# Projected attention before a gated feed-forward layer: two-head blocks per visit, or one head at a time through block-diagonal operands

## Chip, core and metric

The kernel runs on one core of one Trainium2 chip. The metric is the device time of one execution in microseconds (us). Before the change the median of three runs is 549.61 us (547.75 to 552.11).

The core has five engines that work through their own instruction queues in order and wait for each other through semaphores: TensorE (PE, matmuls), ScalarE (ACT), VectorE (DVE), GpSimd (POOL) and SyncE (SP). In this kernel POOL issues the loads that change the type from fp32 to bf16, and SP issues the stores of the output and the transposing transfers ("turns").

## What is computed

```python
# q, k, v: [8 batches, 8 heads, 1024 tokens, 64]; E, F: [64, 1024]
k_proj = E @ k                                    # per batch and head, [64, 64]
v_proj = F @ v                                    # [64, 64]
scores = q @ k_proj.T / 8                         # [1024, 64]
attn = exp(scores - max) / (sum(exp(scores - max)) + 1e-9)
x = attn @ v_proj                                 # [1024, 64]; heads side by side: [8192, 512]
gate = sigmoid(x @ w_gate)                        # w_gate, w_val: [512, 1536]
out = (gate * (x @ w_val)) @ w_out                # w_out: [1536, 512]; out: [8192, 512]
```

The kernel leaves out the subtraction of the maximum; the scores of these inputs are small.

## The kernel before

**Tiling.** A batch is 1024 tokens. The attention works on two token halves of 512 laid over each other: a tile has 128 partitions, 64 for each half, and 512 columns. `Qb` holds q with tokens on partitions; four transposing transfers (`transpose_q`, one for each pair of heads `r`) make `qT`, with the 64 features of the two halves on 128 partitions. `eT` are the exponentials, with the 64 projected positions on partitions. `xT` is the attention's result with features on partitions; the feed-forward part reads it as its moving operand. It has one buffer for even and one for odd batches. A batch of the feed-forward part is two blocks of 512 tokens, and each block three pieces `K`, so a batch has six.

**Feed-forward part.** Each piece runs a chain for the gate (`g_chain`, banks GA and GC of PSUM) and one for the value (`v_chain`, VA and VC); each block ends with a chain for the output matrix (`o_chain`, OA and OC). The chains use a scheme with seven products for a two by two block matrix, with sums of operands prepared by DVE (`xs_sums`, `s_sums`). Their matmuls have 128x128 weights and 256 columns. Partial results are kept by ACT and added by DVE. The output tile `ost` has one buffer for each of four token groups. `evac` and `add_snap` write it, `stored` sends it to DRAM from SP in two pairs, and the next chain's `evac` has to wait until its pair has landed.

**Attention of batch b+1 beside the feed-forward part of batch b.** Four kinds of visit are put in between:

- `sc_visit`: scores of two head pairs, 64x64 blocks of the array, four matmuls of 512 columns beside each other, on banks GA, GC, XA and XB; ACT takes the exponential of each bank.
- `den_visit`: sums of the exponentials over the projected positions, by matmuls with a selection matrix (`dsel8`) on XA; DVE takes two reciprocals of 128x128 (L984) into `rdr`, a piece of `xu`.
- `spread`: SP writes the reciprocals to DRAM (L1153), and four transfers from POOL (L1168) read them back, each value repeated over 64 partitions, into `rb`, another view of `xu`.
- `xo_visit`: the outputs of two head pairs, again in 64x64 blocks; DVE multiplies each bank of 128x512 by the spread reciprocals and writes `xT` (`scaled`, L1184).

`next_kv` projects k and v for the batch after next on XA. `keep_kd` copies the projected k twice side by side, a transposing transfer puts it on both partition halves (`kpD`), and `vd_one` copies the projected v into each half of one of two `vpD`. `next_loads` then loads q, k and v of a later batch.

**What sets the order.** From the last part of batch 0 on, each operation is a task with an estimated duration, and matmuls that belong together form a group with a due time (`goal`). `arranged` replays the tasks with these durations and writes out one order for each engine. On the chip each engine follows this order and waits where a semaphore says so. A transfer that waits in SP's order holds back all that stand behind it.

Batches 0 and 1 run in other ways at the start of the kernel; the change leaves their mathematics as it is. The helpers through which all operations pass have single lines: matmuls are L378, activations L382, loads L396.

Of the kernel before, what the change touches and what calls it, by code (L numbers as in the profile page):

```python
# [12 lines left out]
P = 128  # L13
# [219 lines left out]
def bass_linformer_attn__then__ffn_glu_sigmoid_kernel(  # L233
# [18 lines left out]
    with contextlib.ExitStack() as es:  # L252
# [11 lines left out]
        def within(shape, dtype):  # L264
# [40 lines left out]
        kpd = sbuf("kpd", [64, H, 2, DH], BF16)  # L305
        kpD = sbuf("kpD", [P, H, DH], BF16)
        vpDs = [sbuf(f"vpD{i}", [P, H, DH], BF16) for i in range(2)]
        vpD = vpDs[0]
# [17 lines left out]
        rb = xu[:, :, :].rearrange("p n c -> p (n c)").rearrange(  # L326
            "p (r j h c) -> p r j h c", j=4, h=2, r=2
        )
        rdr = xu[:, 7, 0:256]
# [328 lines left out]
        def keep_v(bks, c0, engines, R=None):  # L658
            vv = vpD[:, :, :].rearrange("p (r h) d -> p r h d", h=2)
            width = 256 if R is None else 128  # L660
            for n, (h, g) in enumerate(((0, 0), (1, 1), (0, 1), (1, 0))):
                o = vv[64 * g : 64 * g + 64, pairs(R), h, :]
                i = bank[bks[h]][64 * h : 64 * h + 64, c0 : c0 + width].rearrange(
                    "p (r d) -> p r d", d=DH
                )
                ws = [("vpD", h, g, x, 0) for x in both(R)]
                if engines[n] == "ACT":
                    act(o, i, [], ws, b=bks[h])
                else:
                    dve(lambda e, o=o, i=i: e.tensor_copy(o, i), [], ws, b=bks[h])  # L670
# [24 lines left out]
        def VPD(R, n=0):  # L695
            return [("vpD", h, g, R, n) for h in range(2) for g in range(2)]
# [203 lines left out]
        def keep_kd(bk):  # L900
            act(
                kpd[:, :, :, :],
                bank[bk][0:64, :]
                .rearrange("p (h d) -> p h d", h=H)
                .unsqueeze(2)
                .to_broadcast([64, H, 2, DH]),
                [],
                ["kpd"],
                b=bk,
                t=0.95,  # L910
            )
# [3 lines left out]
                    kpD[:, :, :],  # L915
                    kpd[:, :, :, :].rearrange("p h g d -> p (h g d)"),
                ),
                r=["kpd"],
                w=[("kpD", 0), ("kpD", 1)],
                dma="kpD",  # L920
            )

        def vd_one(bk, g, n=1):
            act(
                vpDs[n][64 * g : 64 * g + 64, :, :].rearrange("p h d -> p (h d)"),
                bank[bk][64:128, :],
                [],
                [("vpD", h, g, R, n) for h in range(2) for R in range(2)],
                b=bk,
            )  # L930

        rd_v = [nc.dram_tensor(f"rd{b}", [P, 256], FP32, kind="Internal").ap() for b in range(B)]
        group = plan.group
        rb_keys = [("rb", c, rnd) for c in range(2) for rnd in range(2)]

        def attention(b):
# [44 lines left out]
            def rec(c):  # L981
                cc, bk = slice(c * P, (c + 1) * P), den_bank[0]
                dve(
                    lambda e: e.reciprocal((rden if b < 2 else rdr)[:, cc], bank[bk][:, cc]),  # L984
                    [],
                    [("rden", c, R) for R in range(2)] if b < 2 else [("rdr", c)]
                    + rb_keys
                    + ([("xu", n) for n in range(8)] if b == 2 else []),
# [57 lines left out]
            def xo_one(r, bks):  # L1046
                for g in range(2):
                    n = 2 * r + g
                    for c in range(2):
# [4 lines left out]
                            vpDs[(b - 1) % 2][kk, 2 * r + c, :],  # L1054
                            eT[kk, n, :],
                            VPD(r // 2, (b - 1) % 2) + [("eT", n)],
# [93 lines left out]
            def spread():  # L1150
                add(
                    "SP",
                    lambda e: e.dma_start(rd_v[b], rdr),  # L1153
                    r=[("rdr", c) for c in range(2)],
                    w=[("rd", b)],
                    dma="rd",
                    t=2.5,
                )
                for rnd in range(2):
                    for c in range(2):  # L1160
                        src = (
                            rd_v[b]
                            .rearrange("(g m) (o c) -> o g m c", g=8, o=1)[:, :, 2 * rnd + c, :]
                            .to_broadcast([64, 8, 256])
                        )
                        add(
                            "POOL",
                            lambda e, src=src, rnd=rnd, c=c: e.dma_start(  # L1168
                                rb[64 * c : 64 * c + 64, rnd, :, :, :].rearrange(
                                    "p j h c -> p (j h) c"  # L1170
                                ),
                                src,
                            ),
                            r=[("rd", b)],
                            w=[("rb", c, rnd), ("spread", c, rnd)],
                            dma=f"rb{c}{rnd}",
                            t=8.0,
                            )

            def scaled(r, g, bk):  # L1180
                n = 2 * r + g
                rnd, j = n // 4, n % 4
                dve(
                    lambda e: e.tensor_tensor(  # L1184
                        xT[s][:, r, :, 256 * g : 256 * g + 256],
                        bank[bk][:, :].rearrange("p (f c) -> p f c", f=2),
                        rb[:, rnd, j, :, :],
                        ALU.mult,
                    ),
                    [("rb", c, rnd) for c in range(2)],  # L1190
                    [("xT", s, r, 0, g), ("xT", s, r, 1, g)],
                    b=bk,
                )

            def sc_visit(goal, rs, banks):
                with group(goal, 0.22 * len(rs) + 0.2):
                    for i, r in enumerate(rs):
                        sc_one(r, banks[2 * i : 2 * i + 2])
                for i, r in enumerate(rs):
                    for g in range(2):  # L1200
                        exp_half(r, g, banks[2 * i : 2 * i + 2])

            def xo_visit(goal, rs, banks):
                with group(goal, 0.22 * len(rs) + 0.2):
                    for i, r in enumerate(rs):
                        xo_one(r, banks[2 * i : 2 * i + 2])
                for i, r in enumerate(rs):
                    for g in range(2):
                        scaled(r, g, banks[2 * i + g])

            def den_visit(goal, bk):
                den_bank.clear()
                with group(goal, 0.64):
                    den8(bk)
                rec(0)
                rec(1)
                spread()
# [6 lines left out]
                sc_visit=sc_visit,  # L1224
                xo_visit=xo_visit,
                spread_keys=[("spread", c, rnd) for c in range(2) for rnd in range(2)],
                den_visit=den_visit,
# [621 lines left out]
        start_loads()  # L1849
        constants()  # L1850
# [150 lines left out]

        def next_kv(b, goal):
            with group(goal, 1.83):
                kv(b, XA)
            keep_kd(XA)
            vd_one(XA, 0, (b - 1) % 2)
            vd_one(XA, 1, (b - 1) % 2)
# [9 lines left out]
        transpose_q([("kpD", 0)])  # L2017
# [10 lines left out]
        def next_loads(b, marker):  # L2028
            if b < B:
                load_q(b, (), marker)  # L2030
                load_k(b, [("kpD", 0), ("kpD", 1)], marker)
                load_v(b, (), marker)

        for b in range(1, B):
            n = attention(b + 1) if b + 1 < B else None
            late_ = 1 if b == 1 else 0
            more = b + 2 < B
            for u in range(6):
                K = 6 * b + u
                t0 = when(K)  # L2040
                if n is not None:
                    if b == 1 and u == 0:
                        for r in range(NR):
                            n["sc_visit"](9.0 + 3.0 * r, (r,), (XA, XB))
                        n["den_visit"](21.0, XA)
                        transpose_q(n["spread_keys"])
                    if b > 1 and u == 0:
                        n["sc_visit"](t0 - 1.0, (0, 1), (GA, GC, XA, XB))
                        if more:
                            transpose_q((), (0, 1))  # L2050
                    if b > 1 and u == 1:
                        n["sc_visit"](t0 - 1.0, (2, 3), (GA, GC, XA, XB))
                        if more:
                            transpose_q((), (2, 3))
                        n["den_visit"](t0 + 3.0, XA)
                    if u == late_ + 3:
                        if b > 1 and more:
                            next_kv(b + 2, t0 - 5.0)
                            next_loads(b + 3, n["spread_keys"])
                        n["xo_visit"](t0 - 1.0, (0, 1), (GA, GC, XA, XB))  # L2060
                        if b == 1:
                            next_kv(3, t0 + 4.0)
                            next_loads(4, n["spread_keys"])
                    if u == late_ + 4:
# [49 lines left out]
```

The softmax here doesn't subtract the row's maximum and nothing guards it: scores larger than these inputs give would overflow.

## Time and profile before

| what | value |
|---|---|
| median time | 549.61 us |
| span of the profiled execution | 545.3 us |
| PE busy | 512.6 us (94%) |
| DVE busy | 405.1 us (74%) |
| ACT busy | 351.6 us (64%) |
| POOL busy | 53.7 us (10%) |
| granted PE clock, mean | 0.977 of full speed |
| bytes moved by DMA | 69.41 MB, 127 GB/s on average |
| software queue (POOL) | 42.47 MB, 50.3% of the 16 DMA engines' time |
| hardware queue (SP) | 26.22 MB, 21.1% |

Busy time of PE is the union of its matmuls, which overlap in a pipeline. The profile's 40 slices are 13.6 us each, with busy time in tenths. A group's line gives the operation, output and inputs by name (pA and pF are PSUM banks, the letter and number of the bank left out), the shape, the count, busy us and mean ns, and the idle time before. A wait is put down to the engine or transfer that ended last. For a transfer the profile has the time from issue to landing.

### The profile page before, as it was taken

To read this page: it belongs to the slowest core of one execution; us is meant where nothing else is said; L and a number is where in the kernel's file an instruction comes from. 1 tells how busy PE (TensorE), PEld (TensorE's weight loads), DVE (VectorE), ACT (ScalarE), POOL (GpSimd) and SP (SyncE) were. 2 spreads that over 40 slices of the span, in tenths; PEclk is the share of its full clock that TensorE was granted. 3 is DMA by queue.
4 is the path that set the end of the run, shared out by engine and by line. 5 is a ranking of instruction groups with operands and counts; after the bars stand their busy time and mean duration, and the time that the engine had idled before them with its cause. 6 is when DMAs were issued, how large, how long until landed. Compare 5 with 4: busy or idle time off the path is not lost.

```text
span 545.3 us, 11320 instructions
## 1 busy us (share of the span) xinstructions
PE 512.6 (94%) x4668; PEld 403.1 (74%) x4677; DVE 405.1 (74%) x670; ACT 351.6 (64%) x644; POOL 53.7 (10%) x76
## 2 busy tenths in 40 slices
PE   5999999996999969999699996999999999999996
PEld 4545546784888748888488884887888888888885
DVE  3648789785697666877568765687797879786874
ACT  2564756872787636867368673686767866676762
POOL 9310200120102010020100201002000100000000
PEclk9999999998999989999899998999999999999999
DMA  9999999999996993459944799246812090111113
GB/s 157 199 200 199 155 213 196 141 208 142 135 230 130 156 238 63 121 87 133 226 74 122 82 150 239 48 128 88 150 44 78 21 191 32 40 40 40 40 40 115
DMA packets 81091, 69.41 MB, mean 127 GB/s; under 512 B 35088, under 2 KB 70160, under 8 KB 81040
## 3 DMA queue, kind: packets, MB, share of 16 engines
q0 software_dynamic: 37440, 42.47, 50.3%
q1 hardware_dynamic: 43600, 26.22, 21.1%
q8 instruction: 36, 0.59, 0.5%
q14 instruction: 15, 0.12, 0.1%
HBM read 72.88 MB, written 17.56 MB: 166 GB/s over the span
## 4 chain that ended last, share of the span: by engine, by line
PE 80%; DMA 13%; DVE 3%; ACT 1%; issue 1%; POOL 1%; SPq 0%; ACTq 0%; DVEq 0%; POOLq 0%
PE pA L378 44%; PE pF L378 36%; DMA out_dram<-ost 7%; DMA KVs<-in_v_dram 2%; DMA xu<-rd 2%; DMA rd<-xu 1%; DVE hT L1814 1%; DVE vsnap L1692 0%; ACT pF L1681 0%; DVE xT L820 0%; DVE ost L1425 0%; DVE hT L1289 0%; DVE xu L984 0%; POOL KVs L396 0%; POOL Qb L396 0%
## 5 line engine op out<-in xcount | busy, mean ns | idle before, releaser
L382 ACT ACTIVATE sig<-pA 128x512 f32<-128x512 f32 x126 | 75.1, 596 | 52.9 <-PE pA L378 52.3
L1768 DVE TENSOR_TENSOR sig<-pF,sig 128x512 f32<-128x512 f32 x84 | 57.8, 689 | 51.8 <-PE pF L378 26.9
L1681 ACT ACTIVATE pF<-pA 128x512 f32<-128x512 f32 x99 | 58.2, 589 | 33.5 <-PE pA L378 29.0
L1692 DVE TENSOR_TENSOR vsnap<-pF,vsnap 128x512 f32<-128x512 f32 x90 | 62.0, 689 | 20.1 <-ACT vsnap L382 11.4
L378 PE MATMUL pF<-wO,hT 128*128 128x256 bf16 (+1 forms) x400 | 58.6, 285 | 0.2 <-issue 0.2
L1814 DVE SCALAR_TENSOR_TENSOR hT<-sig,vsnap 128x512 bf16<-128x512 f32 x84 | 56.9, 683 | 0.9
L382 ACT ACTIVATE vsnap<-pA 128x512 f32<-128x512 f32 x84 | 50.1, 597 | 8.5 <-PE pA L378 7.0
L382 ACT ACTIVATE sig<-sig 128x512 f32<-128x512 f32 x84 | 52.6, 631 | 4.0 <-DVE sig L1768 3.6
L378 PE MATMUL pF<-xS,wV 128*128 128x256 bf16 x360 | 54.6, 275 | 0.1
L378 PE MATMUL pF<-xT,wG 128*128 128x256 bf16 (+1 forms) x257 | 50.4, 317 | 1.6 <-DVE hT L1289 0.8
L378 PE MATMUL pA<-xT,gT 128*128 128x256 bf16 x336 | 51.8, 278 | 0.0
L378 PE MATMUL pF<-xS,wG 128*128 128x256 bf16 x336 | 51.5, 277 | 0.0
L378 PE MATMUL pA<-xT,vT 128*128 128x256 bf16 x336 | 51.0, 275 | 0.0
L382 ACT ACTIVATE sig<-pF 128x512 f32<-128x512 f32 x66 | 39.4, 596 | 15.3 <-PE pF L378 13.4
L378 PE MATMUL pA<-wT,hT 128*128 128x256 bf16 x360 | 48.8, 273 | 0.0
L378 PEld LDWEIGHTS pF<-wO,hT 128*128 128x128 bf16 x402 | 38.5, 98 | 10.3 <-issue 0.8
L378 PEld LDWEIGHTS pF<-xS,wV 128*128 128x128 bf16 x360 | 34.2, 98 | 10.1 <-issue 2.7
L378 PE MATMUL pF<-xT,wV 128*128 128x256 bf16 (+1 forms) x240 | 41.5, 294 | 0.0
L378 PE MATMUL pA<-xS,gT 128*128 128x256 bf16 x168 | 27.1, 287 | 14.6 <-ACT pF L1681 14.6
L1168 POOL DMA_DIRECT2D xu<-rd x24 | 16.5, 702 | 228.6 <-DMA rd<-xu 171.2
L1814 DVE SCALAR_TENSOR_TENSOR hT<-sig,pF 128x512 bf16<-128x512 f32 x42 | 28.7, 683 | 13.6 <-PE pF L378 13.6
L378 PEld LDWEIGHTS pA<-xT,vT 128*128 128x128 bf16 x336 | 31.8, 98 | 9.2 <-ACT sig L382 4.5
(153 smaller groups left out, 920.8 us busy)
## 6 DMA issues: line engine op xcount, KB each, us to landing
out_dram<-ost SPq DMA_DIRECT2D x61, 256.0 KB, 4.0
xu<-rd POOLq DMA_DIRECT2D x24, 512.0 KB, 12.2
Qb<-in_q_dram POOLq DMA_DIRECT2D x7, 1024.0 KB, 23.8
KVs<-in_k_dram POOLq DMA_DIRECT2D x7, 1024.0 KB, 11.6
KVs<-in_v_dram POOLq DMA_DIRECT2D x7, 1024.0 KB, 15.5
wO<-in_moe_w_out_dram POOLq DMA_DIRECT2D x1, 1536.0 KB, 13.1
wG<-in_moe_w_gate_dram POOLq DMA_DIRECT2D x5, 256.0 KB, 18.6
wV<-in_moe_w_val_dram POOLq DMA_DIRECT2D x5, 256.0 KB, 19.2
```

Source lines behind the costliest of these rows:

```text
L378: return add("PE", lambda e: e.matmul(o, lhsT, rhs, **kw), r=r, x=[("bank", b)])
L382: return add("ACT", lambda e: e.activation(o, i, func, scale=scale), r=r, w=w, x=x, t=t)
L1168: lambda e, src=src, rnd=rnd, c=c: e.dma_start(rb[64 * c : 64 * c + 64, rnd, :, :, :].rearrange("p j h c -> p (j h) c"), src,),
L1681: lambda e: e.activation(bank[c][:, :], bank[a][:, :], AF.Copy, scale=1.0),
L1692: lambda e: e.tensor_tensor(o, bank[bk][:, :], o, ALU.add),
L1768: dve(lambda e: e.tensor_tensor(o, bank[bk][:, :], o, ALU.add), [key], [key], b=bk)
L1814: lambda e: e.scalar_tensor_tensor(o, sg.rearrange("p (j c) -> p j c", j=2), 1.0, x.rearrange("p (j c) -> p j c", j=2), ALU.add, ALU.mult,),
```

## The change

The attention of batches 2 to 7 goes head by head. The projected k of a head becomes a block-diagonal 128x128 matrix (`kpB`), one block for each token half, so that one matmul with all of the array gives a head's scores. The exponentials become the weights of the second product, and the projected v, block-diagonal too (`vpB`), is its moving operand of 130 columns: 64 features and a column of ones for each half. So the result has tokens on partitions, with the sum of the exponentials in the column beside the features. DVE takes the reciprocal of the sums (128x4 for each bank) and multiplies, writing bf16 into `xk`. When two heads are done, a transposing transfer from SP turns `xk` into `xT`. The sum matmuls, the way through DRAM and the spread of the reciprocals are gone. Heads use banks XA and XB only. Each head has a due time of its own, 2.9 us after the one before. `kpB`, `vpB` and `xk` lie in the space of `xu`. Q, K and V of a later batch are loaded once all four turns of `xT` have landed.

```diff
-        def keep_kd(bk):
-            act(kpd[:, :, :, :],
-                bank[bk][0:64, :].rearrange("p (h d) -> p h d", h=H)
-                .unsqueeze(2).to_broadcast([64, H, 2, DH]), ...
+        def blocks_ready(n):
+            if n == 0:
+                pool(lambda e: e.memset(kpd[:, :, :, :], 0.0), ...)
+                return
+            was = [("xu", i) for i in range(8)] + [("vpB", n - 1, x) for x in range(2)]
+            pool(lambda e: e.memset(vpB[n - 1], 0.0), w=was + ["preset"])
...
+        def keep_kd(bk, first):
+            for g in range(2):
+                act(kpd[64 * g : 64 * g + 64, :, g, :],
+                    bank[bk][0:64, :].rearrange("p (h d) -> p h d", h=H), ...
             add(
                 "SP",
                 lambda e: e.dma_start_transpose(
-                    kpD[:, :, :],
-                    kpd[:, :, :, :].rearrange("p h g d -> p (h g d)"),
+                    kpB, kpd[:, :, :, :].rearrange("p h g d -> p (h g d)")
                 ),
...
-            def spread():
-                add("SP", lambda e: e.dma_start(rd_v[b], rdr), ..., dma="rd", t=2.5)
-                for rnd in range(2):
-                    for c in range(2):
-                        src = (rd_v[b] ... .to_broadcast([64, 8, 256]))
-                        add("POOL", lambda e, src=src, rnd=rnd, c=c: e.dma_start(...), t=8.0)
-
-            def scaled(r, g, bk):
...
-            def sc_visit(goal, rs, banks):
...
-            def xo_visit(goal, rs, banks):
...
-            def den_visit(goal, bk):
...
+            def normal(h, f, bk):
+                r, c = h // 2, h % 2
+                i = bank[bk][:, 0:260].rearrange("p (k g e) -> p k g e", k=2, g=2)
+                rc = rcp[:, h % 2, f, :].rearrange("p (k g o) -> p k g o", k=2, o=1)
+                dve(lambda e: e.reciprocal(rc, i[:, :, :, 64:65]), ..., b=bk, t=0.15)
+                dve(lambda e: e.tensor_tensor(
+                        xk[:, r, f, :, :, 64 * c : 64 * c + 64].rearrange("p g k d -> p k g d"),
+                        i[:, :, :, 0:64],
+                        rc.to_broadcast([P, 2, 2, 64]),
+                        ALU.mult), ..., b=bk, t=0.42)
+
+            def head(h, goal, gap, x0, x1):
+                with group(goal, 0.215):
+                    mm(x0, bank[x0][:, :], kpB[:, h, :], qT[:, h, :], ["kpB", ("qT", h // 2)])
+                act(eT[:, h, :], bank[x0][:, :], ..., func=AF.Exp, scale=SCALE)
+                with group(goal + gap, 0.23):
+                    for f, bk in ((1, x0), (0, x1)):
+                        for k in range(2):
+                            j = 2 * f + k
+                            mm(bk, bank[bk][:, 130 * k : 130 * k + 130],
+                                eT[:, h, 128 * j : 128 * j + 128], vpB[b % 2][:, h, :], ...)
+                normal(h, 1, x0)
+                normal(h, 0, x1)
+                if h % 2:
+                    r = h // 2
+                    add("SP",
+                        lambda e: e.dma_start_transpose(
+                            xT[s][:, r, :, :].rearrange("p f (n c) -> p (f n) c", c=P),
+                            xk[:, r, :, :, :, :].rearrange("p f g k x -> p (f g k x)")),
+                        r=[("xk", r, c, f) for c in range(2) for f in range(2)],
+                        w=[("xT", s, r, f, g) for f in range(2) for g in range(2)]
+                        + [("turned", r)],
+                        dma=f"xT{r}")
...
-        def next_loads(b, marker):
+        def next_loads(b):
+            done = [("turned", r) for r in range(NR)]
             if b < B:
-                load_q(b, (), marker)
-                load_k(b, [("kpD", 0), ("kpD", 1)], marker)
-                load_v(b, (), marker)
+                load_q(b, done)
+                load_k(b, ["kpB"] + done)
+                load_v(b, done)
...
+        HEAD = 2.9
         for b in range(1, B):
             n = attention(b + 1) if b + 1 < B else None
+            first = 9.0 if b == 1 else when(6 * b) - 1.0
...
+                if n is not None and u == 0:
+                    for h in range(H):
+                        n["head"](h, first + HEAD * h, 1.6, XA, XB)
+                        if h % 2 and b + 2 < B:
+                            transpose_q((), (h // 2,))
+                    if b + 2 < B:
+                        next_kv(b + 2, first + HEAD * 8)
+                        next_loads(b + 3)
```

## The prediction

> **What bounds the kernel now.** I read the page's slices first, then stretches of 20 us, the timeline round one gap, the waits, and last the DMA issues. In the slices the PE is at 9 nearly everywhere; after start-up there are four dips, each with a dip of the granted clock.
>
> ```profile
> PE   5999999996999969999699996999999999999996
> PEclk9999999998999989999899998999999999999999
> ```
>
> The same in stretches (columns: the stretch, its length, then busy us and instruction count of PE, weight load, DVE, ACT, POOL, then clock, DMA share, GB/s). The first four hold a dip, the last two none.
>
> ```profile
> 120.00:140.00 20.00, 15.11 (x124) 11.03 (x123) 11.45 (x18) 9.40 (x17) 0.00 (x0) 0.91 1.00 132
> 190.00:210.00 20.00, 15.12 (x122) 11.90 (x121) 12.77 (x21) 9.36 (x18) 1.76 (x2) 0.83 1.11 208
> 260.00:280.00 20.00, 14.70 (x117) 11.56 (x115) 11.96 (x20) 8.77 (x16) 1.76 (x2) 0.83 1.07 195
> 330.00:350.00 20.00, 15.56 (x118) 12.57 (x117) 12.01 (x20) 8.59 (x16) 1.01 (x2) 0.83 0.84 160
> 390.00:410.00 20.00, 20.00 (x188) 17.23 (x186) 19.25 (x32) 13.57 (x25) 0.00 (x0) 1.00 0.26 72
> 460.00:480.00 20.00, 20.00 (x186) 17.76 (x185) 16.91 (x30) 13.20 (x26) 0.00 (x0) 1.00 0.14 53
> ```
>
> A full stretch issues about 188 matmuls; the four are short by 64, 66, 71 and 70, together 271. At 20/188 = 0.106 us each that is 28.8 us, 7.2 us a dip: 4.9 us of idle PE, the rest a slow restart. Everywhere else the PE is the bound, with its own work. The timeline of the second dip and the waits say what ends it:
>
> ```profile
> 196.26 0.60 PE L378 MATMUL pF<-xS,wV 128*128 128x256 bf16 x4
> 200.60 0.60 ACT L382 ACTIVATE ost<-pF 128x512 f32<-128x512 f32 x1 [6.82 <-DMA out_dram<-ost]
> 201.74 1.03 PE L378 MATMUL pA<-xS,gT 128*128 128x256 bf16 x4 [4.88 <-ACT pF L1681]
> ...
> ACT ost L382 <- DMA out_dram<-ost: 22.0, 4, 7.2
> DVE xT L1184 <- DMA xu<-rd: 5.7, 1, 5.7
> ```
>
> ACT wants to write `ost` and waits for the previous store of it; ACT works in order, so the seed behind it (L1681), and with it the PE, stand still. Three dips are this wait. The first, near 125, is DVE waiting for the spread reciprocals themselves. What makes a store slow shows in the issues at 174 to 201 and, undisturbed, at 404 to 480:
>
> ```profile
> xu<-rd POOLq DMA_DIRECT2D x4, 512.0 KB, 10.5
> Qb<-in_q_dram POOLq DMA_DIRECT2D x1, 1024.0 KB, 23.8
> out_dram<-ost SPq DMA_DIRECT2D x4, 256.0 KB, 12.9
> kpD<-kpd SPq DMA_TRANSPOSE x1, 14.1
> ...
> out_dram<-ost SPq DMA_DIRECT2D x12, 256.0 KB, 2.4
> ```
>
> A store that takes 2.4 us takes 12.9 beside the 2 MB of broadcast reciprocals (xu<-rd), the Q load behind them and the turning of kpD.
>
> **What the Trainium skill says.** "DMA: Bandwidth & Descriptors", section "Issuing engines are not separate DMA queues": transfers of all issuing engines run on the same 16 DMA engines and interleave. The trace agrees: 2.4 against 12.9 us. "TensorE: Matmul & The Clock Gate", section "Part 1: The HAM clock gate": after an idle window of about 3.4 us the PE restarts at half clock. Agrees: after 4.88 us idle, four 256-column matmuls take 1.03 us instead of 0.60. "VectorE: DVE Perf Modes", section "Walkthrough: the 8-slice pipeline in each mode": reciprocal is an iterated divide. Agrees: 128x128 takes 931 ns, a multiply of 128x512 689, so few elements per reciprocal are worth having.
>
> **The change part by part**, for one of the six batches 2 to 7.
>
> *PE.* Before: two score visits, one sum visit, two output visits. Each is 0.65 us: 218.41 plus six matmuls of 0.109 is 219.06, the visit follows, the next work starts at 219.71.
>
> ```profile
> 218.41 0.82 PE L378 MATMUL pF<-wO,hT 128*128 128x256 bf16 x6
> 219.16 0.40 PE L378 MATMUL pA<-qT,kpD 64*64 64x512 bf16 x1
> 219.71 0.61 PE L378 MATMUL pA<-xT,vT 128*128 128x256 bf16 x4
> ...
> 13.49 0.62 PE L378 MATMUL pA<-gT,Qb 128*128 128x128 bf16 x8 [0.41 <-DMA Qb<-in_q_dram]
> ```
>
> The sum and output visits measure the same, so 5 x 0.65 = 3.25. After: 8 scores of 512 columns at 2 x 0.109 = 0.22, and 32 matmuls of 130 columns with fresh weights. The last line prices those: eight of 128 columns, each with its own weights, in 0.62, so (0.62 - 0.22)/7 = 0.057. Sum 1.75 + 1.82 = 3.57. On the path: +0.3 a batch, +1.9 in all.
>
> *DVE.* Gone: two reciprocals 128x128 (0.93) and eight multiplies 128x512. They start every 0.60 us in a row, so 1.9 + 4.8 = 6.7. New: 16 multiplies 128x256, which start every 0.33 us (L857: four in 1.42, one lasting 0.42), and 16 reciprocals of 128x4, which no row shows. Below, the mean of a 128x1 operation, 146 ns; above, 250 with the wait for its result. I take 0.15. Sum 5.3 + 2.4 = 7.7, at most 9.3. Between the first and the last head's outputs the changed program puts 24.3 us of PE work (counted in its order); of the other DVE work there are 20 operations of 0.60 and 4 of 0.87, 15.5 us, and with seven heads' 6.7 that is 22.2 of 24.3 us. It fits, barely. DVE reached 19.25 of 20 us at 390 to 410 with the PE full, so I charge 0.3 us a batch, 2 in all.
>
> *ACT.* The same eight exponentials; one 1.02 us copy of kpd becomes two of 0.6. Hidden: ACT is at 64%.
>
> *Banks.* Visits no longer borrow the G chain's GA and GC; a head uses XA and XB. Score, exponential, outputs and normalising run in series on XA, and PE works in order: 3 to 4 groups of matmuls (1.1 to 2.2 us) stand between a score and its outputs, 1.3 to 2.2 us between these and the next score. An exponential of 0.6 and two reciprocals with a multiply (0.6) fit in.
>
> *DMA.* Gone: the 128 KB write and the 2 MB of broadcasts. New: four turns of 256 KB. A qT turn of that size holds SP 1.3 us and lands in 3.3; nothing else of the batch is then in flight, because Q, K and V of the batch after next now start only when all four turns have landed. The first dip goes: xT is due at the next batch, 25 to 35 us after the last head. The mechanism of the other three goes too, but its wait stays.
>
> *The added wait.* SP takes the turns in order, each behind DVE. Behind the first turn stand the last stores of the previous output chain. Counting from the batch's first score by PE work: head 1 is normalised at about 7.5 us, the turn holds SP to 9, the stores land at 11.5 to 13.5, ACT wants their `ost` at 13.3. Harmless. Later the turn of kpB (issued near 32, with the V load in flight) stands before four stores; the last pair is ready at 36.5 and wanted at 44.4, and the PE bears 1.9 us more (ready 194.9, PE dry 196.86). With loads alone in flight stores landed in 5.8 to 7.8 us (those issued at 151 to 156), so 43 to 45: no loss. Queued as in the old dips, 12.9 after 37: 50, a loss of 4 and a slow restart. Three batches have such loads at this place; I charge 1 us each.
>
> Sum: 549.6 - 28.8 + 1.9 + 2 + 3 = 527.7.
>
> **Rivals.** *The turns inherit the dip*: kpB and the stores crawl behind the loads. For it: kpD landed after 14.1 us beside software transfers, and the qT turns issued at 44 beside loads took up to 12. Against: 2 MB less in flight, and only V beside kpB. Three dips of 6.5 us remain: 527.7 - 3 + 19.5 = 544. *The head chain becomes the bound* (slower than before): with the DVE at 22 of 24 us, every late multiply delays the next score and the PE behind it. If each of 48 heads waits for one DVE operation more (0.60, with a hand-off some 0.75), 527.7 - 2 + 36 = 562. Against: the slack counted above, and the full stretches of before. *The DMA was hidden anyway* is ruled out by the four dips.
>
> **How the numbers follow.** Forecast 0.69 (518 to 537), dip inherited 0.17, head chain 0.14. Time 527 us. The lower end, 518, is all dips gone and nothing charged but the PE (522.7), less a spread of 4; the upper, 550, takes in the inherited dip and mild cases of the head chain. Under 544.1 (1% less) lie the forecast and half of the second case, 0.78; within 1% 0.09; slower 0.13.
>
> **What would show it.** Right: no PE slice under 9 between 110 and 530 us, no xu<-rd, stores near 45 us after a batch's first score landing within 8 us, xT turns within 5, batches of equal length near 61 us. Wrong: ACT `ost` still waiting for out_dram with 4 us or more; PE waiting for DVE `xu` or for `eT` some tens of times; turns landing after 12 us with SP full of waits.

## The result, and the profile after

The changed kernel takes 523.23 us (median; 522.24 to 524.44), the kernel before 549.61 (547.75 to 552.11). The ratio is 0.952, with a 95% interval of 0.947 to 0.956: 26 us faster. 527 us had been predicted.

The slices of the page after, PE and its granted clock:

```profile
PE   5899999999999999999999999999999999999996
PEclk9799999999999999999999999999999999999999
```

All four dips are gone. (The 8 and the 7 in the second slice are the start of this one execution. Its first `vsnap` store goes out at 78.36 us, where the kernel before has 75.10 and most later runs of the same start-up code 74 to 76.) The same in stretches of 20 us, with the columns shown for before: the stretch, its length, busy us and instructions of PE, weight load, DVE, ACT and POOL, then clock, DMA share and GB/s.

```profile
180.00:200.00 20.00, 19.34 (x176) 16.59 (x174) 15.85 (x26) 14.97 (x28) 2.63 (x3) 1.00 1.09 201
...
240.00:260.00 20.00, 19.99 (x184) 17.51 (x183) 15.91 (x26) 15.58 (x29) 2.62 (x3) 1.00 0.99 188
260.00:280.00 20.00, 20.00 (x189) 17.63 (x187) 14.80 (x30) 13.85 (x27) 0.00 (x0) 1.00 0.54 115
280.00:300.00 20.00, 20.00 (x191) 16.92 (x190) 18.46 (x45) 14.41 (x28) 0.00 (x0) 1.00 0.46 82
```

In the dips the kernel before issued 117 to 124 matmuls in 20 us at a clock of 0.83 to 0.91; now the poorest of these four stretches has 176, at full clock. The DMA issues of 170 to 200 us (operation, count, size, median us from issue to landing) show the stores and the turns that answer to the 12.9 and 14.1 us of before; `xu<-kpd` is the turn of `kpB`:

```profile
out_dram<-ost SPq DMA_DIRECT2D x4, 256.0 KB, 4.8
...
xT<-xu SPq DMA_TRANSPOSE x2, 3.1
...
xu<-kpd SPq DMA_TRANSPOSE x1, 3.1
```

ACT no longer waits for a store of `ost` anywhere. The new work, by groups (busy us, mean ns of one, then idle before it):

```profile
L1170 DVE TENSOR_TENSOR xu<-pA,rcp 128x256 bf16<-128x256 f32 x48 | 20.3, 424 | 0.0
...
L380 PE MATMUL pF<-xu,eT 128*128 128x130 bf16 x96 | 13.3, 220 | 0.0
...
L1163 DVE RECIPROCAL rcp<-pA 128x4 f32<-128x4 f32 x48 | 8.5, 178 | 7.6 <-PE pA L380 7.6
L1163 DVE RECIPROCAL rcp<-pF 128x4 f32<-128x4 f32 x48 | 7.9, 164 | 0.0
```

One place becomes important below. It is the end of a batch's heads on the timeline: the last turn of `xT`, the turn of `kpB`, four stores, and the first sum of the next batch's `xT`:

```profile
240.27 1.23 SPq L1211 DMA_TRANSPOSE xT<-xu  x1
...
241.95 1.23 SPq L927 DMA_TRANSPOSE xu<-kpd  x1
...
243.23 4.04 SPq L1442 DMA_DIRECT2D out_dram<-ost  x4
...
244.28 0.43 DVE L1624 TENSOR_TENSOR xS<-xT 128x512 bf16<-128x512 bf16 x1 [0.78 <-PE pA L380]
```

The sum reads what the turn writes. The turn was issued at 240.27 and landed at 243.34; the sum starts at 244.28, less than 1 us later.

### The profile page after: what moved, and what is told of

The parts are those of the page before. It is cut to its first block, busy times and chain, and to the rows that moved or that the text cites. A ratio compares the mean times of both kernels' runs of the same rounds, so it can differ in the third digit from the quotient of the medians.

```text
span 522.5 us, 11413 instructions
## 1 busy us (share of the span) xinstructions
PE 507.7 (97%) x4629; PEld 413.3 (79%) x4629; DVE 407.9 (78%) x802; ACT 348.7 (67%) x650; POOL 40.3 (8%) x59
## 4 chain that ended last, share of the span: by engine, by line
PE 91%; DMA 3%; DVE 3%; ACT 1%; POOL 1%; issue 0%; DVEq 0%; ACTq 0%; POOLq 0%
PE pA L380 50%; PE pF L380 42%; DMA KVs<-in_v_dram 3%; DVE hT L1813 1%; DMA xT<-xu 1%; DVE vsnap L1691 0%; DVE xT L822 0%; DVE hT L1288 0%; POOL KVs L398 0%; DVE xS L1624 0%; POOL Qb L398 0%; ACT ost L384 0%; ACT sig L384 0%; ACT vsnap L384 0%; ACT vpD L384 0%
## 5 line engine op out<-in xcount | busy, mean ns | idle before, releaser
L1813 DVE SCALAR_TENSOR_TENSOR hT<-sig,pF 128x512 bf16<-128x512 f32 x42 | 28.8, 685 | 31.7 <-PE pF L380 31.6
L380 PE MATMUL pA<-xT,gT 128*128 128x256 bf16 x336 | 50.5, 273 | 0.7 <-ACT sig L384 0.6
L380 PE MATMUL pF<-xS,wG 128*128 128x256 bf16 x336 | 50.4, 273 | 0.0
L384 ACT ACTIVATE sig<-pF 128x512 f32<-128x512 f32 x66 | 39.5, 599 | 15.7 <-PE pF L380 13.8
L380 PEld LDWEIGHTS pF<-wO,hT 128*128 128x128 bf16 x402 | 38.7, 98 | 10.6 <-issue 0.8
L380 PEld LDWEIGHTS pA<-wT,hT 128*128 128x128 bf16 x360 | 34.7, 98 | 4.8
L384 ACT ACTIVATE eT<-pA 128x512 bf16<-128x512 f32 x59 | 34.5, 595 | 4.8 <-PE pA L380 4.6
L380 PEld LDWEIGHTS pA<-xT,gT 128*128 128x128 bf16 x336 | 30.9, 98 | 8.3 <-issue 1.9
## 6 DMA issues: line engine op xcount, KB each, us to landing
wO<-in_moe_w_out_dram POOLq DMA_DIRECT2D x1, 1536.0 KB, 12.5
```

The lines of the kernel that those rows point to most:

```text
L380: return add("PE", lambda e: e.matmul(o, lhsT, rhs, **kw), r=r, x=[("bank", b)])
L384: return add("ACT", lambda e: e.activation(o, i, func, scale=scale), r=r, w=w, x=x, t=t)
L1813: lambda e: e.scalar_tensor_tensor(o, sg.rearrange("p (j c) -> p j c", j=2), 1.0, x.rearrange("p (j c) -> p j c", j=2), ALU.add, ALU.mult,),
```

## The experiments

All ratios are to the kernel before, with their 95% intervals.

| run | edit | us | ratio |
|---|---|---|---|
| a1_late_loads | before, Q and K loads later | 548.03 | 1.000 (0.997 to 1.003) |
| a2_no_spread | before, no spread | 518.37 | 0.946 (0.939 to 0.954) |
| c1_no_kp_turn | before, no turn of kpD | 542.69 | 0.987 (0.979 to 0.996) |
| c4_turn_before_spread | before, turn, then spread | 548.89 | 0.999 (0.996 to 1.002) |
| a3_free_loads | after, loads not gated | 557.93 | 1.019 (1.009 to 1.029) |
| a4_traffic_free_loads | after, not gated, 2 MB more | 556.43 | 1.014 (1.004 to 1.024) |
| d1_free_loads_late_sums | after, not gated, sums of xT later | 541.54 | 0.987 (0.980 to 0.995) |
| c2_traffic_after_turn | after, 2 MB more behind the loads | 522.94 | 0.953 (0.945 to 0.960) |
| d2_traffic_ahead_of_loads | after, 2 MB more after the turns | 522.73 | 0.952 (0.946 to 0.958) |
| c3_traffic_at_turn | after, 2 MB more beside the turns | 547.23 | 0.997 (0.994 to 1.000) |
| d3_dve_half | after, one DVE instruction more a head | 522.00 | 0.953 (0.946 to 0.961) |
| d4_dve_full | after, two DVE instructions more a head | 532.38 | 0.970 (0.964 to 0.976) |

### What made the dips of before: spread, loads, or turn

**The loads held back (a1).**

```diff
-                    [("xT", s, r, 0, g), ("xT", s, r, 1, g)],
+                    [("xT", s, r, 0, g), ("xT", s, r, 1, g), ("fin", r, g)],
...
-                load_q(b, (), marker)
+                load_q(b, [("fin", r, g) for r in range(NR) for g in range(2)], marker)
```

`next_loads` also moves behind the last `xo_visit`.

> The kernel before with one edit: from batch 2 on, Q, K and V of the later batch are loaded only after the attention outputs have been multiplied, so that the 2 MB of spread reciprocals and these loads are no longer in flight together; the order of the PE is the same. Theory (three of the four dips are a store that crawls because spread and loads are in flight together): those three dips go, the one near 125 us, which waits for the spread itself, stays: 549.6 - 3 x 7.2 = 528 us. Rival 1 (the spread alone is enough to slow the stores): the three dips stay or shrink little, 543 to 550 us. Rival 2 (the gain of the change is the head-by-head form, not the transfers): no change, 549 us.

The time is the same, as rival 1 has it, but not because nothing moved. The planner made another order of the work for this run (the expectation says otherwise), and the dips shifted. Three stretches of a1, in which the kernel before has 189, 158 and 151 matmuls, and a wait that is new:

```profile
140.00:160.00 20.00, 16.66 (x140) 12.28 (x132) 12.78 (x22) 8.50 (x16) 2.66 (x3) 0.91 1.02 182
...
180.00:200.00 20.00, 19.56 (x181) 15.22 (x177) 15.88 (x26) 14.48 (x26) 4.35 (x6) 1.00 0.91 175
200.00:220.00 20.00, 20.00 (x188) 17.24 (x186) 16.16 (x29) 14.74 (x28) 0.88 (x1) 1.00 0.97 175
...
DVE xT L1184 <- DMA Qb<-in_q_dram: 2.1, 1, 2.1
```

The second dip is gone. A new one stands before it, where a multiply of `xT` waits until Q has landed: the condition that holds Q back works in this direction too. So the equal times are a gain and losses. The issues of 235 to 268 us, where the third dip has become deeper:

```profile
xu<-rd POOLq DMA_DIRECT2D x4, 512.0 KB, 14.4
KVs<-in_v_dram POOLq DMA_DIRECT2D x1, 1024.0 KB, 24.2
out_dram<-ost SPq DMA_DIRECT2D x4, 256.0 KB, 14.9
KVs<-in_k_dram POOLq DMA_DIRECT2D x1, 1024.0 KB, 9.8
kpD<-kpd SPq DMA_TRANSPOSE x1, 18.4
```

Q is out of this stretch, and the stores still take 14.9 us. The edit was weaker than its expectation says: V waits for its buffer alone, and started at 244.58, while the spread was in flight. So here the run excludes the Q load as a necessary part, not all loads. At the second dip no load at all is beside the spread: there the stores take 10.6 us and the turn of kpD 13.3. That no dip follows is in part the other order, with 151 matmuls instead of 132 between the two writes of `ost` on either side (183.09 and 200.06).

**The spread taken out (a2).** The call of `spread()` in `den_visit` is removed.

> The kernel before without the spread of the reciprocals: neither the write of 128 KB nor the four broadcast transfers; the outputs are multiplied by whatever lies in that space, so the normalisation is left out. All matmuls, exponentials, reciprocals and multiplications stay, and the loads keep their time. Theory (all four dips come from the 2 MB of broadcasts, and the new form itself costs about 2 us): all dips gone, 549.6 - 28.8 = 521 us, about 2 us under the changed kernel. Rival 1 (the loads are what slows the stores): only the dip near 125 us goes, 542 us. Rival 2 (the gain is the form of the heads): no change, 549 us.

All dips go: 518.37 us. The stores of 225 to 245 us, beside a V load, a turn and, at their end, a K load:

```profile
KVs<-in_v_dram POOLq DMA_DIRECT2D x1, 1024.0 KB, 12.0
out_dram<-ost SPq DMA_DIRECT2D x4, 256.0 KB, 7.1
KVs<-in_k_dram POOLq DMA_DIRECT2D x1, 1024.0 KB, 9.8
kpD<-kpd SPq DMA_TRANSPOSE x1, 9.5
```

The loads moved with the edit, since nothing holds them to the spread any more: Q goes out at 221.47 and is not beside these stores. But in a1 V beside the spread leaves the stores at 14.9 us, and here V without it at 7.1, so the difference is the spread. It is what the dips of before need. The old visits alone, without the spread, are not slower than the heads; the gain of the change is not the form of the heads.

**The turn of kpD taken out (c1), and put ahead of the spread (c4).** In nearly every dip the late stores stand behind a turn that has not landed, so I suspected the turn.

```diff
+            if not turn:
+                return
             add(
                 "SP",
                 lambda e: e.dma_start_transpose(
                     kpD[:, :, :],
...
-            keep_kd(XA)
+            keep_kd(XA, b < 4)
```

> The kernel before, with spread and loads kept, and without the turn of kpD from batch 4's on (the later batches score with the k of batch 3, so that part of the result is left out); the K load waits for the spread instead. Theory T, formed after the first four runs (stores crawl because they stand behind a transposing transfer, which needs 12 to 18 us as long as two or more software transfers are in flight beside it): with no turn in front of them the stores land in 6 to 9 us beside the same 2 MB and the same loads, and the dips near 197, 265 and 335 us go: 549.6 - 21.6 = 528 us. Rival B, the one of my prediction (2 MB of broadcasts and a load are enough to slow a store to 13 us): the dips stay, 545 to 550 us.

542.69 us: about 7 of the 22 us expected. Issues of 235 to 268 us, now with no turn in flight:

```profile
xu<-rd POOLq DMA_DIRECT2D x4, 512.0 KB, 14.4
Qb<-in_q_dram POOLq DMA_DIRECT2D x1, 1024.0 KB, 29.5
out_dram<-ost SPq DMA_DIRECT2D x4, 256.0 KB, 13.8
```

The stores still take 13.8 us, beside the spread and the Q load. Theory T falls for the kernel before: the turn adds some us and is not needed. Nor is a load. At the last spread of the kernel before nothing is loaded or turned any more, and spread and stores are alone; issues of 430 to 452 us:

```profile
xu<-rd POOLq DMA_DIRECT2D x4, 512.0 KB, 10.6
out_dram<-ost SPq DMA_DIRECT2D x4, 256.0 KB, 5.1
```

The first of these stores goes out at 444.59 and lands at 450.65, just behind the last piece of the spread (449.47). That is so throughout: in the kernel before, a1, c1 and c4 there are 80 stores that went out while a spread was in flight, and every one landed after the spread's last piece. The rest comes on top: the first of four stores lands 3.9 to 5.0 us behind the spread in the last three dips of the kernel before, 2.2 to 2.5 at the same places without the turn (c1), 1.2 with neither load nor turn. No dip follows the last spread, since little of it is left by then. So a store is slow first of all by what is left of the spread when it goes out. Why it does not get past the spread is not known.

In c4 the turn comes first:

```diff
                     r=[("rdr", c) for c in range(2)]
+                    + ([("kpD", 0)] if 1 < b - 1 < B - 2 else []),
...
+                            next_kv(b + 2, t0 + 1.0)
-                        n["den_visit"](t0 + 3.0, XA)
+                        n["den_visit"](t0 + 3.0, XB)
```

> The kernel before with its visits and its spread, but k and v of the batch after next are projected right after the last scores, the sums go to bank XB, and SP writes the reciprocals only when the turn of kpD has landed: turn first, then spread and loads, with all transfers kept. Theory T: the turn lands in about 3 us, the stores beside spread and loads in 6 to 9 us, the three dips near 197, 265 and 335 us go, the one near 125 stays: about 528 us. Rival B (bytes): dips stay, 545 to 550 us. Rival (the spread now comes some 3 us later and the outputs wait for it): DVE waits for the spread, 535 to 545 us.

Turn first, then spread and loads: 548.89 us, no gain. Issues of 245 to 256 us, and two waits of the whole run:

```profile
out_dram<-ost SPq DMA_DIRECT2D x4, 256.0 KB, 15.1
...
DVE xT L1185 <- DMA xu<-rd: 19.1, 6, 5.7
ACT ost L382 <- DMA out_dram<-ost: 18.4, 3, 8.5
```

The stores are slow without a turn in front, and ACT waits for them 18.4 us (22.0 before). But the wait that the last rival names is there too: DVE waits 19.1 us for the spread, 5.7 before. So the equal time is in part a loss of the edit's own, and c4 bears out c1 by the stores, not by its time. It also has the spread alone once more, at 379 to 404 us, with more of it left: the stores take 8.8 to 13.6 us, ACT waits for one 3.0 us, and PE 1.0. So the spread alone can make a small dip; the larger ones behind late stores, in the kernel before, a1, c1 and c4, all had a load in flight beside it.

### Why the changed kernel has no dips of its own

**The loads not gated (a3), and 2 MB beside them (a4).**

```diff
-            done = [("turned", r) for r in range(NR)]
+            done = []
```

> The changed kernel with one edit: the loads of a later batch no longer wait for the four turns of xT; they start as soon as their buffers are free. Theory (the broadcasts were what made the stores crawl): loads alone let stores land in 6 to 9 us, no dip comes back, 523 to 526 us. Rival (the late loads are what took the dips away): stores crawl again, three dips come back, 540 to 545 us.

557.93 us, slower than the kernel before. PE and DVE instructions stand in the same order as in the changed kernel; one condition on three loads is worth 34.7 us. The page's PE slices, the timeline of the third dip, and the wait behind it:

```profile
PE   5999999997799699995899967999999999999996
...
251.72 1.65 SPq L1211 DMA_TRANSPOSE xT<-xu  x1
253.47 7.39 SPq L927 DMA_TRANSPOSE xu<-kpd  x1
...
264.98 0.42 DVE L1624 TENSOR_TENSOR xS<-xT 128x512 bf16<-128x512 bf16 x1 [10.02 <-DMA xT<-xu]
...
DVE xS L1624 <- DMA xT<-xu: 33.1, 4, 10.0
```

Q was issued at 249.68 and V at 252.13. Beside them the last turn of `xT` takes 13.0 us instead of 3.1, and that of `kpB` 14.2. DVE stands for 10 us before the sum, although PE wants it only for the next batch: DVE works in order, and all that stands behind the sum waits too.

a4 has, besides, four transfers of 512 KB that nothing reads.

```diff
+            for i in range(4):
+                src = rows.rearrange("(g o) c -> o g c", o=256)[i : i + 1, :, :].to_broadcast([64, 8, 256])
+                add("POOL", lambda e, src=src, i=i: e.dma_start(sink[i][:, :, 0:256], src),
+                    r=[("xk", 3, 0, 0)], w=[("sink", i)], dma=f"sink{i}", t=8.0)
```

> The changed kernel with its loads not gated, as in the run before, and with 2 MB of transfers that nothing reads, put in when the attention of a batch nears its end: four of 512 KB from the software queue, DRAM to DRAM, in pieces of 1 KB, each 64 times the same 8 KB, as the spread had them. Theory (2 MB of broadcasts beside the Q load are what delays a store, whatever the form of the heads): some dips come back; three to five of about 3 to 7 us, 535 to 550 us. Rival (the dips belonged to the old order of the work, the visits and the turn of kpD): no dip, 523 to 526 us.

556.43 us: the dips are there, but since a3 has them without the traffic, this run tells nothing about the 2 MB.

**The sums of xT later (d1).**

```diff
                         dma=f"xT{r}",
+                        t=20.0 if r == 3 else None,
```

> The changed kernel with loads that are not gated, as in the run that took 557.9 us, and with one more edit: the planner is told that the last turn of xT takes 20 us instead of 3, so it places the sums of xT (which DVE took 4 us after that turn was issued) some 12 DVE instructions later; nothing else is changed. Theory (in that run the loss was DVE standing in order before a sum that waits for a turn which crawls beside the loads): the wait of xS for xT<-xu goes from 33 us in all to under 8, and 15 to 30 us come back: 528 to 543 us. Rival (the loss was the stores behind the crawling kpB turn, with ACT waiting for ost): 550 us or more.

541.54 us: 16 us come back, and no wait of `xS` for a turn is left. What remains is another wait, which a3 did not have:

```profile
ACT ost L384 <- DMA out_dram<-ost: 19.7, 4, 6.4
```

With DVE free, the stores behind the crawling turn of `kpB` (14.6 us) are the next to be missed: the same wait as before the change. So the 34.7 us have two parts, and the theory held for one.

**The same 2 MB at three places, loads gated (c2, c3, d2).** c3 starts the traffic after head 6, beside the last turns. c2 and d2 let it wait for the turns:

```diff
-                    r=[("xk", 3, 0, 0)],
+                    r=["kpB"] + [("turned", r) for r in range(NR)],
```

> The changed kernel with its loads gated as they are, and with 2 MB of software transfers that nothing reads (four of 512 KB, DRAM to DRAM, pieces of 1 KB), which start when the four turns of xT and the turn of kpB have landed: so 2 MB and the V, K and Q loads run beside the late stores, but beside no turn. Theory T (the turn is what stores crawl behind): stores land in 7 to 12 us, no dip of 4 us or more, 523 to 530 us. Rival B (bytes in flight): stores of 13 us and more, dips return, 535 to 550 us.

> The same changed kernel and the same 2 MB, started some 8 us earlier, after head 6, so that they run beside the last turn of xT and the turn of kpB; the Q, K and V loads stay gated. Theory T: the two turns take 8 to 15 us, the stores behind them land after the kpB turn, dips return: 535 to 550 us, at least 10 us above the run with the later traffic. Rival B: the two runs with the same bytes differ by under 5 us. Rival 3 (only loads of q, k and v, not any software traffic, slow a turn): 523 to 528 us.

c2 took 522.94 us, c3 547.23. c2 alone proves less than it seems: the planner put its traffic behind the V, K and Q loads, and the software queue worked it off in that order, after the stores had landed. d2 puts it ahead of the loads:

```diff
+                tie = [("sink", i) for i in range(4)] if b > 4 else ()
-                load_q(b, done)
+                load_q(b, done, tie)
```

(K and V likewise.)

> The changed kernel, loads gated, with the 2 MB that nothing reads ahead of the V, K and Q loads in the software queue (in the earlier run with this traffic after the turns they stood behind the loads and moved only after the stores had landed); no turn is in flight. Theory B2 (any 2 MB of software transfers in 1 KB pieces slow a store as the spread did, 13 to 17 us): late stores take 12 us or more, ACT waits for ost, 535 to 550 us. Theory S (it was the spread itself, its way of reading and writing, not 2 MB as such): stores land in 6 to 9 us, 522 to 526 us.

522.73 us. Issues of 235 to 268 us:

```profile
sink<-in_k_dram POOLq DMA_DIRECT2D x4, 512.0 KB, 9.0
out_dram<-ost SPq DMA_DIRECT2D x4, 256.0 KB, 5.0
...
xT<-xu SPq DMA_TRANSPOSE x1, 3.0
xu<-kpd SPq DMA_TRANSPOSE x1, 3.1
```

ACT waits once for a store, 2.3 us. d2 and c3 move the same bytes in the same pieces, with the same order of PE, DVE and ACT; in c3 the traffic starts 6 us before the last turn (246.36 and 252.63), in d2 after the turns, and 24.5 us lie between the two. In c3, whose traced execution took 552.65 us, DVE waits for the turns again, and ACT once for a store:

```profile
DVE xS L1624 <- DMA xT<-xu: 19.1, 5, 5.0
...
ACT ost L384 <- DMA out_dram<-ost: 10.3, 1, 10.3
```

That wait ends at 139.66, in batch 2: two stores went out at 126.15 and 129.96 beside the traffic, behind a turn of `xT` that takes 23.0 us, and landed after 12.6 and 9.6 us.

And d2 against c1, with no turn beside the stores in either: in d2 2 MB in rows of 1 KB (packets of 4 KB in both traces) land within 12.8 us (242.80 to 255.60) and leave the stores at 5 us (the two that were issued within them at 6.0 and 8.9; both landed before the last piece of the traffic, as no store beside the spread did); the spread's 2 MB take 24 us (236.27 to 260.25), and the stores 13.8. So it is not 2 MB as such, theory S. What sets the spread apart, writing into 64 partitions of SBUF or reading rows just written, was not tried and stays open.

### How much room DVE has

```diff
+                if f == 0:
+                    y = xk[:, r, f, :, :, 64 * c : 64 * c + 64]
+                    dve(lambda e: e.tensor_tensor(y, y, y, ALU.max), [("xk", r, c, f)], [("xk", r, c, f)], b=bk, t=0.0)
```

d4 has no condition on `f`. The planner counts no time for the new instruction, so the order of the rest stays.

> The changed kernel with one more DVE instruction for each head, on one of its two banks: the maximum of the normalised 128x256 with itself, in place, which changes no value; the order of all other work is the same. From the 128x512 sums in place (0.42 us) I estimate 0.25 us, 0.3 with the hand-off. Theory (DVE has about 2.1 us of room between the first and the last head, as the prediction counted): 7 x 0.3 = 2.1 fits just, 523 to 526 us. Rival (each head waits for its DVE chain): 48 x 0.3 = 14 us more, 537 us.

> The same with the additional DVE instruction on both banks of each head. Theory (2.1 us of room): 14 x 0.3 = 4.2 us between first and last head, 2.1 too many in each of six batches, 13 us: 536 us. Rival (each head waits for its DVE chain): 48 x 0.6 = 29 us, 552 us. Rival 2 (DVE has far more room than counted, because work can slip behind the last head): 523 to 526 us.

One more instruction a head costs nothing that can be measured (522.00 us), two cost 9.2 us (532.38). Their group in d4, and the stretch 280 to 300 us in d3 and then in d4; the line for the changed kernel is above:

```profile
L1186 DVE TENSOR_TENSOR xu<-xu 128x256 bf16<-128x256 bf16 x96 | 28.1, 292 | 3.3
...
280.00:300.00 20.00, 20.00 (x191) 17.44 (x189) 19.73 (x49) 15.23 (x29) 0.00 (x0) 1.00 0.49 101
...
280.00:300.00 20.00, 19.52 (x176) 15.42 (x174) 19.62 (x50) 14.38 (x27) 0.00 (x0) 1.00 0.49 99
```

DVE goes from 18.46 of 20 us to 19.73 with the PE still full (191 matmuls); in d4 it stays at 19.62, and the PE gets to 176. In d4 weight loads and matmuls on the heads' banks wait for the added instruction (us in all, times, longest):

```profile
PEld pA L382 <- DVE xu L1186: 6.7, 17, 0.6
...
PE pA L382 <- DVE xu L1186: 3.6, 11, 0.4
```

The start-up differs from one execution to the next (the traced one of d3 took 527.29 us). From the first to the last write of `ost` by ACT, which leaves it out, the traces have 423.50 us for the changed kernel (95.25 to 518.75), 423.68 for d3 (97.91 to 521.59) and 435.59 for d4 (91.73 to 527.32).

d3 adds 48 x 0.292 / 6 = 2.3 us a batch and loses nothing; d4 adds 4.7 and loses 9.2 / 6 = 1.5 by the medians, 12.1 / 6 = 2.0 by the traces. So the room is between 2.3 and about 3 us a batch. Whether d4 lacks DVE time as a whole, or each head then waits for its own chain, the two runs do not separate.

## Why the prediction was right, and where it was not

**The bound and the gain: right.** Four dips were to go, worth 28.8 us. a2, which takes out only the spread, gains 31.2 (549.61 - 518.37), and 28.7 from the first to the last write of `ost` (450.37 before, 421.69 in a2). Slices, clocks and the missing wait of ACT agree with what the prediction named as signs.

**What causes a slow store: half right.** The step put down the 12.9 us to the spread, the Q load and the turn of kpD together. The spread is needed (a2), and it alone holds a store back until it has landed (430 to 452 us before). Q is not needed (a1), and the turn is not either, though it adds about 7 us in all (c1). The number of bytes alone is not the cause (d2). The stretch of 404 to 480 us was not quite undisturbed: four of its twelve stores are those beside the last spread.

**The charges: 6.9 us charged, less paid.** The medians have 523.23 - 518.37 = 4.9 between a2 and the changed kernel. Of the 6.2 us between their two traced executions, 4.1 lie ahead of the first write of `ost` (91.14 and 95.25), in the start-up; in seven of the eight other traces of the changed start-up code that write comes at 91.1 to 92.6. From the first to the last write a2 takes 421.69 and the changed kernel 423.50: all three charges together come to 1.8 there, in six batches.

**PE +1.9: at most that.** The 1.8 us hold PE's charge and what the other two cost. From write to write of `ost` (180.87, 242.44, 303.14, 363.95) the batches are 61.6, 60.7 and 60.8 us long, as forecast.

**DVE +2: no such cost.** The room of 24.3 - 22.2 = 2.1 us was counted well; d3 and d4 put it at 2.3 to about 3. The reciprocals cost 0.16 to 0.18 us instead of 0.15. But room that isn't used up costs nothing, and d3 spends 2.3 us more without loss. The 0.3 us a batch should have been nought.

**Late stores +3: about 1.** The times by the batch's first score (209.45) came out closely: the turn of kpB at 32.5 (predicted 32), the last pair issued at 36.8 (36.5), landing at 44 to 45.5 (43 to 45). They took 7.1 to 9.4 us, for which within 8 had been said, and nothing waits for them. From the write of `ost` before such stores to the second one after it stand the same 251 matmuls in four batches: 28.40, 27.54 and 27.67 us where loads run beside the stores (from 180.87, 242.44 and 303.14), 27.53 where none does (from 363.95). That is 1.0 us more in all, 0.6 of it one wait of PE for ACT. That the stores cause this was not tested alone.

**The step that failed, without harm.** The prediction has it that `xT` is due at the next batch, 25 to 35 us after the last head. PE's use is; but the planner had put the first sum of `xT` into DVE's order 4 us behind the last turn, and the order, not the use, is what a late turn meets. The order of the changed kernel could have been read for this ahead. The rival "turns inherit the dip" is real too. In d1, with loads not gated and the sums out of the way, ACT waits for stores behind the crawling turn of kpB, and the run lies 541.54 - 523.23 = 18.3 us above the changed kernel, near the 19.5 that the rival was given. In a3 the wait of the sum stands in its place, which no rival named, and the loss is 34.7. What keeps both away is the gate on the loads, which the prediction named only in passing, for the reason that nothing else would be in flight. A cost of the gate does not show: Q, loaded at 246.60, has landed at 266.51, and its first turn is issued at 274.55.

**xT turns within 5 us: nearly.** They landed in 3.0 to 5.1 us, except the first three of batch 2, which run beside K, V and Q loads and took 12.5, 13.0 and 10.1; DVE waits 1.4 us for one, and no dip follows.

**The head chain: rightly a rival, rightly ruled out.** No matmul waited for a link of it, and the weight loads waited for `eT` 0.4 us in all. With one more instruction on each bank it begins to show: in d4 matmuls wait 3.6 us in all for the added one.

A version that beats the changed kernel was not found: a2 is below it, but leaves out the normalisation; all other runs are level with it or slower.

## What to carry to other kernels

When a transfer on the critical path is taken out and another put in, ask what will be in flight beside the new one, and give loads with time to spare a condition that keeps them away: here that condition is worth 34.7 us, more than the whole gain. A tensor is due where its first reader stands in its engine's order, not where its value is used; a planner that believes in 3 us for a transfer puts a reader behind it that stops the engine when it takes 13. And two transfers of the same size and pieces are not alike: measure the one that you have, and check in the trace that an added transfer really moved when it was meant to.

## What the runs showed of the hardware that was not expected

- A turn of 256 KB lands in 3.1 us alone and in 13.0 to 14.2 beside two loads of 1 MB from the software queue (a3). SP was held up to 7.4 us by the issue of one (the line at 253.47), against 1.23 alone.
- 2 MB copied from DRAM to DRAM in rows of 1 KB, with no turn in flight, leave the stores beside them at 6.0 and 8.9 us (d2), where the spread of the same size makes them 13.8 (c1).
- A store that was issued while the spread was in flight never landed before the spread's last piece: 80 of 80 in the kernel before, a1, c1 and c4, with nothing else in flight too (444.59 to 450.65 against 449.47).
- Transfers of the software queue were worked off in the order of their issue: the traffic that stood behind three loads of 1 MB did not move before the stores had landed at 251.41 (c2).
